# One ring of SBUF slots for all large operands of a cached-attention decode kernel

## The chip, the cores and the metric

The kernel runs on one core of a Trainium2 chip. The metric is the device time of one execution in microseconds (us), lower is better. A time is quoted as the median of some runs. An execution is called slow when it is over 1.5% above the fastest of the same kernel.

Engines: PE is TensorE (PEld its weight loads), DVE is VectorE, ACT is ScalarE, POOL is GpSimd, SP is SyncE, which issues the large loads. "Group" means four batches of one kv head: 1 MB of K and 1 MB of V; there are 16. "The Trainium skill" is a set of notes on the chip; its pages are named by title.

## The reference, cut to what matters

One decode step: layer norm, attention over the last 1024 positions of a cache, a gated FFN beside it, and a product of both added to the input.

```python
B, D, Hq, Hkv, Sk, Dh, F = 8, 512, 32, 8, 4096, 128, 1792      # W = Sk // 4 = 1024
xn = layernorm(x)                                   # x: (8, 1, 512), all bfloat16
q = xn @ wq                                         # wq: (512, 4096)
scores = einsum(q, k[:, :, Sk-W:, :]) * Dh ** -0.5  # four q heads share a kv head
o = einsum(softmax(scores), v[:, :, Sk-W:, :])
s = o @ wo                                          # wo: (4096, 512)
g = silu((gelu(xn @ w_gate) * (xn @ w_up)) @ w_down)
return x + s * g
```

Nothing is used twice: 16 MiB of K, 16 of V, 4 each of wq and wo and 5.25 of FFN weights are read once, 47.46 MB. So the time of the loads is a floor for any version.

## The kernel before

Weights have tiles of their own. K goes through 6 buffers of 256 KB, V through 20. All of K comes first, then all of V; the probabilities of all 64 (head, batch) pairs wait in SBUF between. In both caches a partition takes 8 consecutive positions of one pair, a row of 2 KB.

```python
k_pool = ctx.enter_context(tc.tile_pool(name="k_pool", bufs=6))
v_pool = ctx.enter_context(tc.tile_pool(name="v_pool", bufs=20))
# ... wq, gate, up and down loads; q projection and FFN ...
for hkv in range(Hkv):
    for b in range(B):
        k_sb = k_pool.tile([P, NSC, Dh], BF16, name="k_sb")            # NSC = 8
        nc.sync.dma_start(out=k_sb, in_=A_k_cache[b, hkv, win0:Sk, :]
                          .rearrange("(p c) d -> p c d", c=NSC))
        # 8 transposes into kT_ps (PE), one copy to kT (DVE),
        # 8 score matmuls (PE), one exp into pT_all (ACT)
# 4 matmuls with ones and reductions: the sums of all exps; one reciprocal
for hkv in range(Hkv):
    for b in range(B):
        v_sb = v_pool.tile([P, NSC, Dh], BF16, name="v_sb")
        nc.sync.dma_start(out=v_sb, in_=...)                           # as K
        # 8 matmuls into oT_ps (PE), one product with the reciprocal (DVE)
    nc.sync.dma_start(out=wo_sb[:, hkv * rep : (hkv + 1) * rep, :], in_=...)  # 512 KB
    # 4 matmuls of 512 columns into s_ps
```

The softmax here doesn't subtract the row's maximum and nothing guards it: scores larger than these inputs give would overflow.

## Time and profile before

| what | value | view |
|---|---|---|
| time, median of the first 3 runs | 150.45 us (149.07 to 153.27) | runs |
| HBM read | 47.46 MB, 318 GB/s over the span | page |
| last stage, V and wo | DMA share 1.02 to 1.06, 355 to 385 GB/s | windows |
| K stage, 40 to 90 us | DMA share 0.84 to 1.00, 273 to 349 GB/s | windows |

DMA share is the time of the packets as a share of 16 DMA engines; above 1, packets overlap. The page cuts the span into 40 slices, counted here from 0. A digit is the busy share of a slice in tenths; PEclk is the clock granted to PE, in tenths of full speed; the last row is what the DMA engines moved.

```profile
PE   0000137499988896998998996597474748585760
...
DVE  2100001057296885788788885831211121121213
...
PEclk9999999999999999689999999755555555555555
DMA  4999999957999699889989899999999999999900
GB/s 117 430 419 416 407 403 372 372 161 212 315 390 368 211 342 325 252 278 298 298 321 323 263 311 309 393 372 378 372 380 371 376 357 380 337 386 380 349 30 2
```

There are three stages. Up to 23 us PE waits for wq while the DMA is full. From slice 9 on PE and DVE are busy with K, and the loads mostly drop below 350 GB/s. From slice 25 on V and wo stream with a full DMA, and PE is idle for about a third of the time. SP's waits say why the loads drop in the middle (issuing line, what it waited for, us in total, times, longest):

```profile
SPq L203 <- PE sc_ps L221: 21.0, 31, 1.0
...
SPq L203 <- PE kT_ps L211: 7.7, 19, 1.3
```

K loads wait for the matmuls that free one of six buffers, 28.7 us in all. So the loads are the floor, and they are held back in the K stage. The chain of waits agrees (the chain that ended last, shares of the span; SPq is SyncE's instruction queue, "issue" is time without a visible wait):

```profile
DMA 66%; PE 24%; DVE 5%; issue 3%; SPq 1%
```

### The profile page before, as it was taken

The page shows a single profiled execution, that of the slowest core. Times are in us where ns is not written, and L with a number is a line of the kernel's source. Part 1 is how long each engine was busy: PE and PEld are TensorE (multiplying, and loading weights), DVE is VectorE, ACT ScalarE, POOL GpSimd, SP SyncE. Part 2 cuts the span into 40 slices and gives each one's busy share as a digit, 9 for nine tenths or more (in the row PEclk, how much of TensorE's full clock was granted, in tenths as well). Part 3 has the DMA queues.
Part 4 walks back from the last instruction along what each step waited for, and adds up shares of the span by engine and source line. Part 5 has one row for each costly group of instructions (what it writes and reads, how often), then busy time and mean ns, then how long its engine had stood idle before and what let it go on. Part 6 is the DMA issues. An engine that isn't in the chain of part 4 may idle for free.

```text
span 149.5 us, 4236 instructions
## 1 busy us (share of the span) xinstructions
PE 97.0 (65%) x1830; PEld 73.4 (49%) x1830; DVE 64.2 (43%) x154; ACT 16.5 (11%) x70; POOL 1.4 (1%) x6
## 2 busy tenths in 40 slices
PE   0000137499988896998998996597474748585760
PEld 0000127497466785987876874453433334342420
DVE  2100001057296885788788885831211121121213
ACT  4000000052122221222222221000000000000000
POOL 3000000000000000000000000000000000000000
PEclk9999999999999999689999999755555555555555
DMA  4999999957999699889989899999999999999900
GB/s 117 430 419 416 407 403 372 372 161 212 315 390 368 211 342 325 252 278 298 298 321 323 263 311 309 393 372 378 372 380 371 376 357 380 337 386 380 349 30 2
DMA packets 25843, 47.74 MB, mean 319 GB/s; under 512 B 2256, under 2 KB 8160, under 8 KB 25312
## 3 DMA queue, kind: packets, MB, share of 16 engines
q1 hardware_dynamic: 23216, 41.97, 79.9%
q10 hardware_dynamic: 2336, 3.67, 7.1%
q0 software_dynamic: 272, 1.84, 2.9%
q8 instruction: 14, 0.23, 0.6%
q14 instruction: 5, 0.04, 0.1%
HBM read 47.46 MB, written 0.01 MB: 318 GB/s over the span
## 4 chain that ended last, share of the span: by engine, by line
DMA 66%; PE 24%; DVE 5%; issue 3%; SPq 1%
DMA v_sb<-in_A_v_cache_dram 22%; DMA k_sb<-in_A_k_cache_dram 17%; DMA wq_sb<-in_A_wq_dram 15%; DMA wo_sb<-in_A_wo_dram 12%; PE kT_ps L211 10%; PE s_ps L300 4%; PE sc_ps L221 4%; DVE kT L217 3%; PE qT_ps L135 2%; PE f_ps L181 2%; PE gu_ps L153 1%; SPq L269 1%; DVE tmp L309 0%; DVE out_sb L311 0%; SPq L292 0%
## 5 line engine op out<-in xcount | busy, mean ns | idle before, releaser
L217 DVE COPY kT<-kT_ps 128x1024 bf16<-128x1024 bf16 x64 | 43.6, 690 | 14.4 <-PE kT_ps L211 14.1
L211 PE MATMUL kT_ps<-ident,k_sb 128*128 128x128 bf16 x512 | 41.6, 228 | 3.2 <-DMA k_sb<-in_A_k_cache_dram 3.2
L211 PEld LDWEIGHTS <-k_sb 128*128 128x128 bf16 x512 | 31.3, 102 | 3.8 <-DMA k_sb<-in_A_k_cache_dram 3.8
L284 DVE TENSOR_TENSOR oT_all<-oT_ps,recip_all 128x4 bf16<-128x4 f32 x64 | 11.0, 175 | 36.4 <-PE oT_ps L277 35.4
L277 PE MATMUL oT_ps<-pT_all,v_sb 128*128 128x4 bf16 x512 | 19.9, 167 | 10.2 <-DMA v_sb<-in_A_v_cache_dram 7.3
L277 PEld LDWEIGHTS <-v_sb 128*128 128x128 bf16 x512 | 16.8, 105 | 19.4 <-DMA v_sb<-in_A_v_cache_dram 10.6
L221 PE MATMUL sc_ps<-qT_all,kT 128*128 128x4 bf16 x512 | 22.7, 166 | 3.8 <-DVE kT L217 1.7
L221 PEld LDWEIGHTS <-kT 128*128 128x128 bf16 x512 | 17.9, 97 | 10.0 <-DVE kT L217 8.5
L300 PE MATMUL s_ps<-wo_sb,oT_all 128*8 128x512 bf16 x32 | 14.9, 620 | 8.0 <-DMA wo_sb<-in_A_wo_dram 8.0
L228 ACT ACTIVATE pT_all<-sc_ps 128x32 bf16<-128x32 f32 x64 | 12.6, 197 | 43.9 <-PE sc_ps L221 43.9
L153 PE MATMUL gu_ps<-xnT_sb,wg_sb 128*128 128x8 bf16 x56 | 3.4, 168 | 12.5 <-DMA wg_sb<-in_B_w_gate_dram 10.4
L142 DVE CAST qT_all<-qT_ps 128x64 bf16<-128x64 f32 x4 | 0.9, 225 | 21.3 <-PE qT_ps L135 21.3
L300 PEld LDWEIGHTS <-oT_all 128*8 128x8 bf16 x32 | 3.3, 106 | 12.8 <-issue 10.3
L153 PEld LDWEIGHTS <-wg_sb 128*128 128x128 bf16 x56 | 2.7, 104 | 10.5 <-DMA wg_sb<-in_B_w_gate_dram 10.5
L135 PE MATMUL qT_ps<-xnT_sb,wq_sb 128*128 128x8 bf16 x128 | 3.6, 168 | 3.4 <-DMA wq_sb<-in_A_wq_dram 3.4
L135 PEld LDWEIGHTS <-wq_sb 128*128 128x128 bf16 x128 | 3.5, 104 | 3.5 <-DMA wq_sb<-in_A_wq_dram 3.5
L153 PEld LDWEIGHTS <-wu_sb 128*128 128x128 bf16 x56 | 2.6, 104 | 5.2 <-DMA wu_sb<-in_B_w_up_dram 3.0
L153 PE MATMUL gu_ps<-xnT_sb,wu_sb 128*128 128x8 bf16 x56 | 3.1, 168 | 2.9 <-DMA wu_sb<-in_B_w_up_dram 2.9
L163 ACT ACTIVATE z_381<-gu_ps 128x112 f32<-128x112 f32 x1 | 0.3, 264 | 26.8 <-PE gu_ps L153 26.8
L252 DVE TENSOR_REDUCE sums_sb<-sums_ps 128x64 f32<-128x512 f32 x4 | 2.7, 684 | 1.1 <-PE sums_ps L243 1.1
L181 PE MATMUL f_ps<-wd_sb,hT_sb 128*8 128x512 bf16 x14 | 3.2, 379 | 0.0
L120 PE MATMUL xnT_ps<-ident,xhat 8*128 8x8 bf16 x4 | 0.3, 168 | 4.4 <-DVE xhat L99 4.4
(33 smaller groups left out, 15.9 us busy)
## 6 DMA issues: line engine op xcount, KB each, us to landing
k_sb<-in_A_k_cache_dram SPq DMA_DIRECT2D x64, 256.0 KB, 4.3
v_sb<-in_A_v_cache_dram SPq DMA_DIRECT2D x64, 256.0 KB, 6.1
wq_sb<-in_A_wq_dram SPq DMA_DIRECT2D x1, 4096.0 KB, 22.0
wo_sb<-in_A_wo_dram SPq DMA_DIRECT2D x8, 512.0 KB, 6.2
wg_sb<-in_B_w_gate_dram ACTq DMA_DIRECT2D x1, 1792.0 KB, 14.3
wd_sb<-in_B_w_down_dram ACTq DMA_DIRECT2D x1, 1792.0 KB, 32.1
wu_sb<-in_B_w_up_dram POOLq DMA_DIRECT2D x1, 1792.0 KB, 16.9
x_sb<-in_A_x_dram SPq DMA_DIRECT2D x1, 8.0 KB
```

The lines of the kernel that those rows point to most:

```text
L135: nc.tensor.matmul(qT_ps[:, mi, :], wq_sb[:, k, m * Dh : (m + 1) * Dh], xnT_sb[:, k, :], start=(k == 0), stop=(k == NDC - 1),)
L153: nc.tensor.matmul(gu_ps[:, j, w, :], wsb[:, k, j * 128 : (j + 1) * 128], xnT_sb[:, k, :], start=(k == 0), stop=(k == NDC - 1),)
L181: nc.tensor.matmul(f_ps, hT_sb[:, j, :], wd_sb[:, j, :], start=(j == 0), stop=(j == NFC - 1),)
L211: nc.tensor.transpose(kT_ps[:, c * 128 : (c + 1) * 128], k_sb[:, c, :], ident,)
L217: nc.vector.tensor_copy(out=kT, in_=kT_ps)
L221: nc.tensor.matmul(sc_ps[:, c, :], kT[:, c * 128 : (c + 1) * 128], qg, start=True, stop=True,)
L228: nc.scalar.activation(out=pT_all[:, gi, :, :], in_=sc_ps, func=ACT.Exp, scale=inv_sqrt_dh,)
L252: nc.vector.tensor_reduce(out=sums_sb[:, i * GB : (i + 1) * GB, :], in_=sums_ps.rearrange("p (g c j) -> p g j c", g=GB, c=NSC, j=rep), axi ...
L269: nc.sync.dma_start(out=v_sb, in_=A_v_cache[b, hkv, win0:Sk, :].rearrange("(p c) d -> p c d", c=NSC),)
L277: nc.tensor.matmul(oT_ps, v_sb[:, c, :], pT_all[:, gi, c, :], start=(c == 0), stop=(c == NSC - 1),)
L284: nc.vector.tensor_tensor(out=oT_all[:, hkv * rep : (hkv + 1) * rep, b], in0=oT_ps, in1=recip_all[:, gi, :], op=ALU.mult,)
L300: nc.tensor.matmul(s_ps, oT_all[:, h, :], wo_sb[:, h, :], start=(h == 0), stop=(h == Hq - 1),)
```

## The change

Its intent: keep the DMA queue full from the first to the last byte, with long rows. Every large operand goes through one ring of 22 slots of 1 MB in order of use. A K or V slot holds four batches; partition `r * 4 + i` takes 32 consecutive positions of batch `i`, a row of 8 KB. K and V alternate by group. As a slot mixes four batches, a score matmul gives columns for all four, and exps with a bias of -30000 wipe out the wrong ones, one exp for each batch. FFN weights come in rows of 7 KB with their columns taken at a stride of seven. The output and the FFN's second product are spread over four groups of 32 partitions. The core of the diff, shortened, with cuts at `# ...`:

```diff
-    k_pool = ctx.enter_context(tc.tile_pool(name="k_pool", bufs=6))
-    v_pool = ctx.enter_context(tc.tile_pool(name="v_pool", bufs=20))
+    ring = ctx.enter_context(tc.tile_pool(name="ring", bufs=22))
+    p_pool = ctx.enter_context(tc.tile_pool(name="p_pool", bufs=3))
+    I = 4; R = P // I; C = W // R; CB = 8; NB = C // CB        # C = 32, NB = 4
+    # ...
+    def load_cache(src, g):
+        # ... hkv and b0 from g
+        t = slot()
+        nc.sync.dma_start(out=t, in_=src[b0 : b0 + I, hkv, win0:Sk, :]
+                          .rearrange("i (r c) d -> r i (c d)", c=C))
+    # ...
+    load_k(0); load_wq(); load_k(1); load_v(0); load_k(2); load_v(1); load_ffn()
+    for g in range(3, NG):
+        load_k(g)
+        load_v(g - 1)
+        if g % GW == 0:
+            load_wo(g // GW - 1)
+    load_v(NG - 1)
+    load_wo(NG // GW - 1, parts=2)
+    # ...
+    def score_block(n):        # 8 matmuls of 16 columns; after a group's last block:
+            for i in range(I):
+                nc.scalar.activation(
+                    out=pT[g][:, :, i * rep : (i + 1) * rep],
+                    in_=sc[g][:, :, i * rep : (i + 1) * rep],
+                    func=ACT.Exp, bias=diag[:, i : i + 1], scale=inv_sqrt_dh)
+    def sum_group(g):
+        sums_ps = ps_m.tile([P, C, IR], FP32, name="m_ps")
+        nc.tensor.matmul(sums_ps, ones_pp, pT[g], start=True, stop=True)
+        # reduce, reciprocal (DVE)
+    def value_block(g, s):
+        if s == 0:
+            sum_group(g)
+            oT[g] = ps_m.tile([P, IR], FP32, name="m_ps")
+        # 8 matmuls into oT[g]; after the last block the product with the reciprocal
+    # ...
+    LA = 2
+    for n in range(NG * NB):
+        if n + LA < NG * NB:
+            transpose_block(n + LA)
+        score_block(n)
+        g, s = n // NB, n % NB
+        if g > 0:
+            value_block(g - 1, s)
+        # ... ffn_up() at g == 3, ffn_down() at g == 4, project_out() in two of every four g
```

## The prediction

> **What bounds it now.** Three stages, by the table of windows. Up to 23 us it waits for wq: the DMA moves 378 to 412 GB/s with large rows, PE is nearly idle. From 30 to 86 us it transposes K; only 225 to 349 GB/s flow, because loads wait for one of six K buffers (SyncE's waits: 31 waits, 21.0 us, for the score matmuls, 19 more for transposes), while DVE (7.7 to 8.5 of each 10 us) and PE pace each other: 0.8 us per (head, batch). From 95 to 144 us V and wo stream with the DMA share above 1.0, but at 355 to 385 GB/s. The chain of waits says the same: DMA 66%, PE 24%, DVE 5%. Overall 47.5 MB are read in 149.5 us: 318 GB/s.
>
> **What changes.** The bytes stay. (a) One ring of 22 MB, in order of use: a load waits for the use of a slot 22 loads older, so the queue should never run dry. (b) Rows: the trace's DMA packet records give medians of 46 ns for 1 KB, 84 ns for 2 KB, 275 ns for 7 KB, 319 ns for 8 KB; over 16 engines that is 356, 390, 417 and 411 GB/s. K, V and wq come in 8 KB rows, FFN weights in 7 KB rows; only wo keeps 1 KB. The Trainium skill (DMA: Bandwidth & Descriptors, Rules for kernel authors) asks for 128 partitions and at least 1 MiB per DMA; the 256 KB loads here already kept the share above 1.0 in the V stage, so I credit row length, not DMA size. (c) K and V interleave, so PE and DVE work spreads over the whole stream.
>
> **DMA time.** 37.7 MB at 411 = 91.8 us; FFN 5.5 MB at 417 = 13.2; wo 4.2 MB at 356 = 11.8: 116.8 us.
>
> **Does compute fit?** Per group (2 MiB, 5.1 us of DMA), estimates from trace pitches at full clock: 32 transposes at 57 ns, 32 scores and 32 value matmuls at 28 ns, one sum: about 3.9 us of PE. DVE: four kT copies of 690 ns, one reduce of 684 ns, reciprocal and product about 0.4: 3.85 us. ACT: four exps of about 0.3. All fit, at about 75%. At half clock PE would need some 6.5 us, but it is then continuously busy and should recover full clock, as in the K stage, which ran mostly at 1.0. The FFN's weight columns are now read at a stride of seven; if that slows weight loads to 150 ns, 17 us of PE appear while PE has slack, and the ring hides it.
>
> **Ends.** Head 2.5 us to the first data (x landed then). Tail: today 5.7 us from the last wo landing. Now 16 tiled matmuls (about 1.5), two 128x128 vector operations (0.6 instead of 1.4), four small stores (2.8), semaphore 0.4: about 5.3 us.
>
> **Sum.** 2.5 + 116.8 + 5.3 = 124.6; I say 124.5 us, range 120 to 131. Faster by over 2%: 0.97; same 0.02; slower 0.01.
>
> **Signs.** DMA share near 1.0 and 405 to 420 GB/s in every slice from 3 us to about 119, dips only for wo; SyncE's waits mostly for DMA landings, hardly for PE; the chain nearly all DMA, ending in wo, project-out, store; PE idle but for gaps; PE clock mostly 1.0 after about 40 us.
>
> **What would make it wrong.** 8 KB rows slower because four batches 8 MiB apart are read in turn (then under 400 GB/s at full share); PE or DVE lagging, through a cold clock or strided weight loads, until the ring fills (SyncE waits on PE, DMA share drops); or a backlog of compute after the last landing. Faster, to 120: 8 KB rows above 420 GB/s.

## The result, and the profile after

The changed kernel took 139.34 us (median of 4, 137.75 to 140.10), the kernel before 151.45 us in the same job. The ratio is 0.920, with a 95% interval of 0.910 to 0.931. (A ratio is the mean time of one kernel's fast runs over that of the other's of the same rounds, so not quite the ratio of the medians quoted.) So it is faster, but by less than half of what was predicted: 124.5 us was said, 131 at most.

The profiled run took 140.1 us, and so counts as slow. Nothing below rests on it alone: the profile of e3, a fast run with the same issue order but for the moved FFN, shows the same waits, the same 2.77 us for 24 transposes and about the same pace (6.58 us from sum to sum, mean of six intervals from 90.85 to 130.33 us).

```profile
PE   0486189692006999987696876977596969696960
...
DVE  3443018473003403749374663647283936383741
...
PEclk9999999959555555699868698569755777777775
DMA  3999999999999999999999999999999999200000
GB/s 116 424 429 419 424 419 427 413 423 409 425 422 419 407 376 418 417 417 417 417 386 389 419 422 424 417 417 371 406 417 417 415 414 345 96 5 0 5 0 5
```

The loads do what was predicted. The DMA row is full, the rate is 407 to 429 GB/s but for the slices with wo and their neighbours, and it never runs dry. In the packet records an 8 KB packet took 316 ns on average over all such packets, 415 GB/s over 16 engines. A slice is 3.46 us, so the last load ends in slice 34 (at 120.1 us by the packet records). But the span is 138.3 us, and PE is still at work for most of the rest. The chain of waits has turned over:

```profile
PE 47%; DMA 29%; ACT 10%; DVE 8%; issue 2%; SPq 1%; ACTq 0%
```

DMA fell from 66% to 29%, PE rose from 24% to 47%, and ACT, absent before, has 10%. PE's own waits show what ACT does there (engine, line, what it waited for, us, times, longest):

```profile
PE m_ps L282 <- ACT pT L270: 14.5, 13, 1.4
PE kT_ps L248 <- DMA slot<-in_A_k_cache_dram: 10.0, 2, 9.7
```

L282 is the matmul that sums a group's exps. It waits for them in 13 groups, about 1.1 us each. The second line is one long wait for K 3 while the FFN weights come. The timeline of one group shows the steps (start, duration, engine, line, operation, count, idle time before it). L248 are transposes, L260 scores, L295 values:

```profile
124.73 0.35 PE L295 MATMUL m_ps<-pT,slot 128*128 128x16 bf16 x8
...
124.97 1.14 ACT L270 ACTIVATE pT<-sc_ps,diag 128x128 bf16<-128x128 f32 x4 [5.19 <-PE sc_ps L260]
...
126.16 0.59 PE L282 MATMUL m_ps<-pT,ones_pp 128*128 128x512 bf16 x1 [1.08 <-ACT pT L270]
...
126.54 2.77 PE L248 MATMUL kT_ps<-ident,slot 128*128 128x128 bf16 x24
...
131.36 1.14 ACT L270 ACTIVATE pT<-sc_ps,diag 128x128 bf16<-128x128 f32 x4 [5.25 <-PE sc_ps L260]
...
132.55 0.38 PE L282 MATMUL m_ps<-pT,ones_pp 128*128 128x512 bf16 x1 [1.09 <-ACT pT L270]
```

From sum to sum this group takes 6.39 us; the mean over the 11 intervals from 61.14 to 132.55 us is 6.49. Its loads take about 5.1 us (2 MiB at 415 GB/s). Two things stand out. The sum stands directly behind the last values of the group before, when its exps have just begun. And the 24 transposes behind the sum take 2.77 us, or 107 ns apart (2.77 less one matmul of 0.31, over 23), where the K stage of before had 57 ns (eight weight loads in 0.46 us). The PEclk row shows why: mostly 5 to 8 from slice 10 on. The clock records of this trace alternate between 1.0 and 0.5 in stretches of 3.4, 6.8, 10.2 or 23.9 us.

The program states another order: transposes of two blocks ahead, scores, values, eight by eight, with the sum in front of the first values. But the layer that builds the program may reorder what does not depend on each other. This is what it issues on PE for one group in steady state (from the built program, and the same in the trace; weight loads left out):

```
 1 sum of group g          <- exps of group g
24 transposes of K g+1     (three blocks)
 8 scores   8 transposes   16 scores
24 values of group g
 8 scores                  -> the exps of group g+1 can start
 8 values of group g
 1 sum of group g+1        <- waits for the exps of group g+1
```

### The profile page after: what moved, and what is told of

Read it like the earlier page. It is cut to its first block, busy times and chain, and to the rows that moved or that the text cites. A ratio compares the mean times of both kernels' runs of the same rounds, so it can differ in the third digit from the quotient of the medians.

```text
span 138.3 us, 4349 instructions
## 1 busy us (share of the span) xinstructions
PE 97.6 (71%) x1984; PEld 89.1 (64%) x1984; DVE 64.8 (47%) x135; ACT 21.7 (16%) x70; POOL 1.3 (1%) x8
## 4 chain that ended last, share of the span: by engine, by line
PE 47%; DMA 29%; ACT 10%; DVE 8%; issue 2%; SPq 1%; ACTq 0%
DMA slot<-in_A_k_cache_dram 29%; PE kT_ps L248 22%; ACT pT L270 10%; PE sc_ps L260 7%; PE m_ps L295 6%; DVE kT L252 5%; PE m_ps L282 4%; PE m_ps L333 4%; PE s_ps L317 2%; DVE sums L284 2%; SPq L84 1%; DVE recip L288 1%; SPq L101 0%; DVE tmp L405 0%; DVE out_sb L407 0%
## 5 line engine op out<-in xcount | busy, mean ns | idle before, releaser
L248 PEld LDWEIGHTS <-slot 128*128 128x128 bf16 x512 | 46.0, 130 | 25.1 <-issue 12.7
L248 PE MATMUL kT_ps<-ident,slot 128*128 128x128 bf16 x512 | 52.5, 283 | 10.0 <-DMA slot<-in_A_k_cache_dram 10.0
L270 ACT ACTIVATE pT<-sc_ps,diag 128x128 bf16<-128x128 f32 x64 | 18.4, 368 | 86.3 <-PE sc_ps L260 81.5
L260 PE MATMUL sc_ps<-qT_all,kT 128*128 128x16 bf16 x512 | 21.9, 173 | 2.6 <-DVE kT L252 2.0
L260 PEld LDWEIGHTS <-kT 128*128 128x128 bf16 x512 | 19.7, 102 | 3.8 <-DVE kT L252 3.1
L284 DVE TENSOR_REDUCE sums<-m_ps 128x16 f32<-128x512 f32 x16 | 11.1, 691 | 18.7 <-PE m_ps L282 18.7
L295 PE MATMUL m_ps<-pT,slot 128*128 128x16 bf16 x512 | 18.1, 171 | 0.2 <-issue 0.2
L282 PE MATMUL m_ps<-pT,ones_pp 128*128 128x512 bf16 x16 | 7.6, 476 | 14.6 <-ACT pT L270 14.5
L295 PEld LDWEIGHTS <-slot 128*128 128x128 bf16 x512 | 15.9, 98 | 1.8 <-issue 1.7
L304 DVE TENSOR_TENSOR oT_all<-m_ps,recip 128x16 bf16<-128x16 f32 x16 | 3.6, 228 | 10.3 <-PE m_ps L295 10.2
L228 PE MATMUL m_ps<-xnT_sb,slot 128*128 128x8 bf16 x128 | 4.1, 169 | 4.8 <-DMA slot<-in_A_wq_dram 4.7
L228 PEld LDWEIGHTS <-slot 128*128 128x128 bf16 x128 | 3.7, 104 | 5.7 <-DMA slot<-in_A_wq_dram 5.7
L333 PE MATMUL m_ps<-xpT_sb,slot 128*128 128x8 bf16 x112 | 6.1, 194 | 0.0
L333 PEld LDWEIGHTS <-slot 128*128 128x128 bf16 x112 | 6.1, 152 | 0.0
L288 DVE RECIPROCAL recip<-sums 128x16 f32<-128x16 f32 x16 | 4.0, 252 | 0.5
## 6 DMA issues: line engine op xcount, KB each, us to landing
slot<-in_A_wq_dram SPq DMA_DIRECT2D x4, 1024.0 KB, 11.4
```

Source lines behind the costliest of these rows:

```text
L228: nc.tensor.matmul(q_ps[:, h, :], wq_t[k][:, h * Dh : (h + 1) * Dh], xnT_sb[:, k, :], start=(k == 0 and h == 0), stop=(k == NDC - 1), skip ...
L248: nc.tensor.transpose(t_ps[:, c * P : (c + 1) * P], k_t[g][:, cc * Dh : (cc + 1) * Dh], ident)
L260: nc.tensor.matmul(sc[g][:, s * CB + c, :], kT[n][:, c * P : (c + 1) * P], qT_all[:, hkv, b0 : b0 + I, :], start=True, stop=True,)
L270: nc.scalar.activation(out=pT[g][:, :, i * rep : (i + 1) * rep], in_=sc[g][:, :, i * rep : (i + 1) * rep], func=ACT.Exp, bias=diag[:, i : ...
L282: nc.tensor.matmul(sums_ps, ones_pp, pT[g], start=True, stop=True)
L284: nc.vector.tensor_reduce(out=sums, in_=sums_ps.rearrange("p c m -> p m c"), axis=AX.X, op=ALU.add)
```

## The experiments

Three theories were put against each other. ORDER: the issue order makes PE wait for the exps in every group. CLOCK: PE gets a low clock whatever the order, and that is what costs. IDLE: the 10 us of waiting while the FFN weights come are what is missing at the end. DVE's pace was a further rival. Eleven runs were made, in three jobs on three chips (e1 to e4, e5 to e8, e10 to e12), each with its own runs of the kernel before. Between jobs compare ratios. (The record calls e5 to e8 "unclear" against the kernel before, although their intervals lie below 0.95; three of the seven runs of before in that job were slow.)

| run | us | ratio to before | PE clock, profiled run |
|---|---|---|---|
| changed kernel | 139.34 | 0.920 | 0.759 |
| e1 program order | 127.10 | 0.845 | 0.844 |
| e2 sum late | 128.28 | 0.851 | 0.826 |
| e3 FFN late | 137.32 | 0.913 | 0.780 |
| e4 one exp | 130.08 | 0.866 | 0.841 |
| e5 warm | 131.88 | 0.875 | 0.915 |
| e6 program order, 2 KB rows | 133.88 | 0.888 | 0.856 |
| e7 changed kernel, 2 KB rows | 140.74 | 0.931 | 0.766 |
| e8 program order, no wait for exps | 131.37 | 0.872 | 0.826 |
| e10 sum late, exps twice | 128.82 | 0.855 | 0.811 |
| e11 changed kernel again | 140.11 | 0.927 | 0.712 |
| e12 program order again | 127.37 | 0.845 | 0.855 |

The profiles of e10 and e11, like that of the changed kernel, fell on slow runs. The two fast runs of the changed kernel had clocks of 0.78 and 0.80.

### e1: PE in program order

```diff
+    def mm(*args, **kw):
+        return tc.keep_in_program_order(nc.tensor.matmul(*args, **kw))
+    def tr(*args, **kw):
+        return tc.keep_in_program_order(nc.tensor.transpose(*args, **kw))
-                nc.tensor.matmul(            # every matmul and transpose alike
+                mm(
```

> All TensorE instructions kept in the order in which the program states them (transposes of two blocks ahead, scores, values, eight by eight), nothing else changed. Theory ORDER (the time over the DMA comes from the order in which the built program issues a group: sum behind the last scores, so PE waits for four exps of 1.14 us, then 24 transposes in a lump at a cold clock): the wait of the sum for the exps falls from 14.5 us to under 8, PE's clock stays above 0.85 after 50 us, a group takes about 5 us instead of 6.3, and the time falls to 122 to 130 us. Rival CLOCK (PE gets the low clock whatever the order, because it is idle too often): clock still 0.55 to 0.85, time above 134. Rival DVE pace: DVE busy near 9 of 10 us, time above 132.

Measured: 127.10 us, ratio 0.845 (0.840 to 0.850). No instruction was added or taken away; the results are right. The page and PE's waits:

```profile
PEclk9999999999555555555999999997569999999975
DMA  3999999999999999999999999999999999999600
GB/s 115 388 439 423 417 420 423 425 414 423 409 429 420 420 420 366 412 417 415 417 420 412 394 378 418 425 423 415 417 410 371 406 420 425 415 417 388 213 20 5
```

```profile
PE kT_ps L36 <- DMA slot<-in_A_k_cache_dram: 14.5, 4, 13.7
...
PE m_ps L33 <- ACT pT L276: 5.9, 11, 1.1
```

A slice is now 3.14 us, and the last packet of the loads ends at 120.0 us, where it ended before; the program now ends at 125.6 us instead of 138.3. The wait for the exps is 5.9 us instead of 14.5, and the clock is 9 from slice 19 on but for three slices in the middle and the last two. The mean time from sum to sum is 5.00 us (64.92 to 119.87 us in 11 intervals), the pace of the loads. PE has caught up with the loads again late in the run: the chain of e1 holds a K load from 94.38 us that lands 13.22 us later, and PE waits for it. DVE did the same work (64.7 us busy against 64.8), so its pace was not what bound. ORDER stands, and CLOCK as an independent cause falls: the order alone brought most of the clock back. One part of the expectation failed: the clock was to stay above 0.85 after 50 us, and it was 0.54 from 50 to 60 us and 0.83 in two later stretches of 10 us (1.00 in the other four to 120 us). In the first of these PE was busy nearly all the time, so a PE that is busy by the profile is not enough for full clock (stretch, its length, busy us of PE, PEld, DVE, ACT and POOL, then PEclk, DMA share, GB/s):

```profile
50.00:60.00 10.00, 9.91 (x180) 9.47 (x179) 4.27 (x11) 1.70 (x6) 0.00 (x0) 0.54 1.04 413
```

### e2: the sum stated later

```diff
         if s == 0:
-            sum_group(g)
             oT[g] = ps_m.tile([P, IR], FP32, name="m_ps")
         ...
         if s == NB - 1:
+            sum_group(g)
```

> Only the sum of a group is stated after its value matmuls, so that it no longer stands directly behind the exps; the lump of 24 transposes stays. ORDER, wait part alone: the 14.5 us that the sum waits for the exps go to under 2, and if nothing takes their place the time falls by 10 to 14 us, to 125 to 129. If the lump of transposes at the low clock is the larger part, or the freed wait turns into another one (value matmuls waiting for the exps), it falls by under 6 us, to 134 or more.

Measured: 128.28 us, ratio 0.851 (0.844 to 0.858). In the built program a sum stands in the same place, but it is now that of the group whose values have just ended, not of the group whose exps have just begun; the 24 transposes still come in a lump.

```profile
PE kT_ps L248 <- DMA slot<-in_A_k_cache_dram: 13.3, 2, 13.1
PE sc_ps L260 <- DVE kT L252: 6.5, 19, 0.5
```

No wait of the sum for the exps is left (0.9 us in one place, for values). So the wait, with what follows from it, is enough to explain nearly all of what e1 gained, and the lump of transposes is harmless once PE does not stand still in front of it: from sum to sum it takes 5.12 us (62.20 to 118.50 in 11 intervals).

### e4: one exp in place of four

```diff
-            for i in range(I):
-                nc.scalar.activation(... 128x128 ..., bias=diag[:, i : i + 1], ...)
+            nc.scalar.activation(out=pT[g], in_=sc[g], func=ACT.Exp,
+                                 bias=diag[:, 0:1], scale=inv_sqrt_dh)
```

> One exp over 128x512 with one bias column in place of four of 128x128 (wrong result on purpose; the instruction count of ACT falls by 48). ORDER: the wait of each sum shrinks with the exps, from about 1.15 to about 0.6 us, in some 14 groups: 6 to 9 us less, 130 to 133. CLOCK or DVE: under 3 us less, and the freed time appears as longer transposes.

Measured: 130.08 us, ratio 0.866 (0.858 to 0.873). The order of the built program is that of the changed kernel.

```profile
PE m_ps L281 <- ACT pT L269: 8.3, 13, 0.8
```

The exp takes 0.69 us instead of four of 0.37 that end 1.14 us after the first start, and the sum's wait fell from 14.5 to 8.3 us, 6.2 us. The ratio fell by 0.055, some 8 us, as expected, and the clock was 0.84 in the profiled run, against 0.78 and 0.80 in the fast runs of the changed kernel. The 8 us are more than 6.2, but with an uncertainty of about 2 us they do not show that a shorter wait pays more than its length; e5 tests this. (On purpose this kernel computes the wrong softmax, yet it passed the comparison with the reference, as did e6 and e7. So that comparison cannot tell a right softmax from a wrong one here, and it does not prove the attention of the other kernels right either. The likely reason, not tested, is that the attention enters the output only through a product that is small beside x.)

### e5: useless matmuls in the wait

Here PE's clock is to be changed without touching the order or the wait for the exps.

```diff
         sums_ps = ps_m.tile([P, C, IR], FP32, name="m_ps")
+        # ... s_ps_all is 128x512; s_ps becomes its first 128 columns
+        before = last[0]                       # the last value matmul issued
+        for _ in range(4):                     # from the third group on
+            d = nc.tensor.matmul(s_ps_all[:, P : 4 * P], ones_pp, <128x384 of pT[g - 1]>,
+                                 start=False, stop=False, skip_group_check=True)
+            behind(d, before); before = d      # issue order only
         nc.tensor.matmul(sums_ps, ones_pp, pT[g], start=True, stop=True)   # behind the last
```

> The changed kernel with its issue order as it is, plus four useless 128x384 matmuls (into spare columns of the accumulator's bank) between the last values and each sum, where PE waits about 1.16 us for the exps; results unchanged. Theory CLOCK FOLLOWS IDLENESS (the wait costs twice: itself, and a low clock for the transposes after it, 104 instead of 57 ns each): PE's clock after 60 us rises from about 0.73 to above 0.9, the 24 transposes behind the sum take under 1.7 us instead of 2.5, and the time FALLS, to 127 to 133, though work was added. Rival WAIT ONLY: the clock stays or does not matter; the added 0.64 us (1.28 us at half clock) fit in the wait, so 137 to 141.

Measured: 131.88 us, ratio 0.875 (0.864 to 0.885), against 0.920 of the changed kernel. Work was added, and 0.046 of the time of before, some 7 us, went away. (The order did not stay quite the same: in the trace the sum of two groups now stands behind 16 matmuls of project_out, and that of a third before six transposes. In 11 groups the sum still waits, 5.7 us in all. At some 0.5 us for 16 such matmuls, the two moved sums cannot make up the 7 us.) One group:

```profile
117.56 0.81 PE L295 MATMUL s_ps_all<-pT,ones_pp 128*128 128x384 bf16 x4
117.60 1.14 ACT L271 ACTIVATE pT<-sc_ps,diag 128x128 bf16<-128x128 f32 x4 [4.50 <-PE sc_ps L261]
...
118.79 0.38 PE L302 MATMUL m_ps<-pT,ones_pp 128*128 128x512 bf16 x1 [0.42 <-ACT pT L271]
...
119.01 1.50 PE L249 MATMUL kT_ps<-ident,slot 128*128 128x128 bf16 x24
```

The exps start at 117.60 and the sum at 118.79 us: the wait is as long as it was, but PE works through two thirds of it. Then 24 transposes take 1.50 us instead of 2.77, and PE's clock is 1.00 in every 10 us from 60 to 120 us. The mean time from sum to sum is 5.75 us (61.13 to 124.43 in 11 intervals) against 6.49. So the standstill costs twice: itself, and a half clock for what follows. WAIT ONLY falls. Not separated is whether the useless matmuls helped by ending the standstill or by being large themselves, with 384 columns beside the 16 of scores and values. The Trainium skill (TensorE: Matmul & The Clock Gate, Part 1) describes this gate: half clock by default, full clock after a busy window of about 3.4 us. The stretches of the clock records, multiples of 3.41 us at 0.5 or 1.0, agree.

### e3: the FFN's weights later

```diff
     load_v(1)
-    load_ffn()
     for g in range(3, NG):
         load_k(g)
         load_v(g - 1)
+        if g == 6:
+            load_ffn()
         # ffn_up() at g == 7, ffn_down() at g == 8 instead of 3 and 4
```

> The FFN's 5.25 MB are loaded after K 6 and V 5 instead of before K 3, and the FFN is computed four groups later. Theory IDLE (PE stood idle from 33 to 42.6 us while FFN weights came, and all after that is bound by compute, so those 10 us add to the end): PE's idle there falls to under 3 us and the time falls by 6 to 10 us, to 129 to 133. If the time after 43 us is bound by the loads instead: within 2 us of 139.

Measured: 137.32 us, ratio 0.913 (0.907 to 0.919), which the interval of the changed kernel overlaps. The expectation of IDLE failed in both numbers: the wait for K shrank by 2.5 us only, and the time by 0.007 of before, about 1 us. This meets the number of the rival, within 2 us of 139, but not its reason: that the loads bind after 43 us does not fit e7 below.

```profile
PE m_ps L283 <- ACT pT L271: 14.5, 13, 1.4
PE kT_ps L249 <- DMA slot<-in_A_k_cache_dram: 7.5, 2, 7.2
```

The wait moved to where the weights went, slices 17 and 18 of its page, 58 to 65 us. While 5.5 MB without K or V come, PE runs dry, wherever that is. So IDLE is not a loss that moving the load can give back. The first line, from a fast run, is the wait of the changed kernel again.

### e6 and e7: rows of 2 KB again

```diff
-            out=t,
+            out=t.rearrange("p (i w) -> p i w", i=I),
-            in_=src[b0 : b0 + I, hkv, win0:Sk, :].rearrange("i (r c) d -> r i (c d)", c=C),
+            in_=src[b0 : b0 + I, hkv, win0:Sk, :].rearrange("i (p c) d -> p i (c d)", p=P),
```

In e6 this is done to e1, in e7 to the changed kernel. A load stays 1 MB.

> e1_program_order with the caches' rows of 2 KB again, in the same 1 MB loads (each partition takes 2 KB of each of the four caches; wrong result on purpose, since the mask of the exps no longer fits the layout). 33.6 MB change rows. Theory DMA BOUND after the order is mended: packets of 84 to 93 ns for 2 KB give 352 to 390 GB/s instead of 415, so 5 to 14 us longer than e1: 132 to 141. If e1 is still bound by compute: within 2 us of e1 (127).

> The changed kernel with 2 KB rows in the same 1 MB loads, order untouched (wrong result on purpose). Theory: after 43 us it is bound by the chain of sums, transposes and exps, not by loads, so slower rows cost only what they delay K 3 (about 40 us at 6 to 15 per cent of the part that changes, 10 MB: 2 us): 139 to 143, less than half of what they cost e1. Rival: bound by loads: as much longer as e6 is than e1.

Measured: e6 133.88 us, ratio 0.888 (0.879 to 0.897), so 0.043 of before or 6.5 us over e1. e7 140.74 us, ratio 0.931 (0.917 to 0.945), so 0.011 or 1.6 us over the changed kernel, whose interval it overlaps. The rates of e7:

```profile
DMA  4999999999999999999999999999999999981000
GB/s 82 392 424 430 388 391 386 406 422 418 417 390 388 387 368 375 388 385 387 382 386 374 368 385 386 384 387 381 377 364 385 386 385 391 378 296 66 5 0 5
```

Both kernels' loads slowed alike, from about 418 to about 386 GB/s in the slices of K and V; by the packet records they end at 127.6 us in e7 and 127.5 in e6, 7.5 us later than with 8 KB rows. Yet e7's time hardly moves, while e6's does. This is the mark of what binds: the changed kernel is bound by PE's chain, e1 by its loads. The long rows are worth 6.5 us, but only after the order is mended.

### e8: no wait for the exps at all

```diff
-        if g > 0:
-            value_block(g - 1, s)
+        if n > NB:                                   # one block later
+            value_block((n - NB - 1) // NB, (n - NB - 1) % NB)
         # and sum_group(g) after the group's last values, as in e2
```

> e1_program_order, but each value block is stated one block later and a group's sum after its values, so no matmul should wait for the exps. In e1 PE waited 5.9 us for exps and the last landing was at about 121 us of 125.6, so if e1 is at the floor of its loads: 126 to 128, no gain over e1 (127.1), with the wait gone and PE idle for K instead. If PE still binds: 122 to 125.

Measured: 131.37 us, ratio 0.872, slower than e1 by 0.027 of before. The expectation failed. The wait for the exps is gone, but others came:

```profile
PE m_ps L33 <- issue: 4.1, 3, 1.5
PE m_ps L33 <- DVE sums L290: 3.5, 12, 0.9
```

Values of the next group now wait for a PSUM buffer that the sum's reduction still holds (12 times), and at the end the sum, its reduction and the product follow the last values instead of running beside them: from the start of the last exps to the last projection it takes 3.93 us (121.65 to 125.58) instead of 2.97 in e1 (118.68 to 121.65). The clock was also lower from 60 to 70 us, 0.62 against 1.00. How the 4 us divide among these was not tested.

### e10: the exps twice, off the path

```diff
-            for i in range(I):
+            for i in [j for j in range(I) for _ in range(2)]:    # on e2
```

> e2_sum_late with every exp issued twice (same result), 18 us more of ACT. If it is where the sum stands that makes the exps cost time, and not the exps' length or ACT's share, the doubled exps (2.3 us per group) still end before the values that need them (which start about 3.6 us after the exps do in e2): within 2 us of e2, ratio to before 0.84 to 0.87. If ACT's time counts wherever the sum stands: 13 groups of 1.15 us, 12 us or more over e2.

Measured: 128.82 us, ratio 0.855 (0.849 to 0.860) against 0.851 of e2. Doubling the exps cost nothing that can be told from noise, where shortening them in e4 had gained some 8 us. The order of PE's matmuls in its trace is that of e2. So it is not ACT's load but the place of the sum that counts.

### e11 and e12: both again on one chip

> The changed kernel again, unaltered, to stand on one chip beside e12 and e10: 137 to 141, as before.

> e1_program_order again, unaltered, on one chip with the changed kernel: 126 to 129, 9 to 13 us less than e11, about 7 to 9 per cent.

Measured: 140.11 us (138.64 to 142.36) and 127.37 us (126.72 to 127.74). One of e11's four runs was slow; by fast runs the ratio is 127.30 / 139.62 = 0.912. Program order beats the changed kernel by 9% and the kernel before by 15.5% (ratio 0.845, 0.839 to 0.850).

## Why the prediction was wrong

It was right that the kernel gets faster, and right about the loads. It said 124.5 us, 120 to 131, and the time was 139.3.

- **Loads: right.** Rows of 8 KB were put at 411 GB/s, and 415 were measured; 7 KB at 417 (415 measured); 1 KB at 356 (328 measured, packets of 50 ns instead of 46, worth 1 us; 46 was a median, and the mean of the same packets before was already 49). The last load was to end at 2.5 + 116.8 = 119.3 us. It ended at 120.1 us, with some luck: the first packet came at 1.7 us, and the loads then took 118.4 us.
- **Head and strided weights: right, or harmless.** The 112 matmuls on FFN weights at a stride of seven took 6.1 us, 55 ns each at half clock, not 17 us. (The record of one weight load is 152 ns long, but they overlap.)
- **DVE and ACT: right.** DVE has four copies of 680 ns, 691 + 252 + 228 ns of reduction, reciprocal and product: 3.9 us for a group, as said. ACT has four exps of 0.37 us.
- **The step that failed: "about 3.9 us of PE ... All fit, at about 75%".** It added up pitches of matmuls as if PE never waited inside a group, and took the order in the source for the order of issue. The built program puts the sum only eight value matmuls behind the scores that its exps need, so PE stood still for about 1.1 us in 13 groups. A group took 6.49 us, more than the 5.1 us of its loads. From 43 us on the loads ran ahead, and the end came some 18 us after the last load instead of 5.3. e1 shortens the wait to 5.9 us and e2 takes it away; they give 127 and 128 us.
- **The second half of that step: "it is then continuously busy and should recover full clock".** PE was not continuously busy, as the standstill came in 13 of the 16 groups. The clock flipped between full and half. e5 shows that this part alone costs about 7 us.
- **What was named as a risk came, by another road.** "PE or DVE lagging, through a cold clock or strided weight loads, until the ring fills" was listed; the lag came from an order that the prediction had not looked at. Of the signs given, the PE clock was not "mostly 1.0", and the chain was not "nearly all DMA". SP's waits on PE were a bad sign: the longest were 11.4 us in the changed kernel and 11.1 us in e1, both with a full DMA all the same.

With the order mended the sum of the prediction holds within 3 us: 127.1 against 124.6. Most of the rest is that the sum counted the profile's span, while the device time is 1.8 us longer (127.39 against 125.6 us in e1's profiled run). Within the span e1's last packet ended at 120.0 us, 119.3 said, and the tail took 5.6 us, 5.3 said.

What stays open: why the clock falls at a standstill of only 1.1 us was not settled, nor why it stayed at 0.54 in e1 from 50 to 60 us with PE busy for 9.91 of 10 us. In e2 the same lump of transposes and scores runs mostly at full clock without the standstill, but how much idle time in a window is too much was not measured.

## What to carry to other kernels

When a kernel is to be bound by its loads, compute per group must fit in the groups' time with its waits, not only by the sum of its instructions: look at what each engine's next instruction in the built order waits for, and do not trust the order in the source. A repeated short standstill of PE may cost twice, as it can drop the clock of what follows. And if faster loads gain nothing, slow them down on purpose: if the time does not move either, the gain is waiting behind something else.

## What the Trainium skill lacked or had wrong

- TensorE: Matmul & The Clock Gate, "Why this matters for your kernels", asks for no idle gaps above about 3 us between bursts. Here standstills of 1.1 us, one in each 6.4 us, with matmuls of 16 columns around them, went with a clock that flips to half; filling them with useless matmuls (e5) brought it from 0.78 and 0.80 to between 0.90 and 0.915 (means of the fast runs), and the ratio to before from 0.920 to 0.875. The page also tells of short idles between groups of matmuls that make the clock oscillate ("A second HAM failure mode: psum-queue depth-cycling"), but gives no length for them.
- The same page, Part 4, says that full clock does not engage for PE transposes. Here runs of 24 transposes took 1.50 us with the clock granted at 1.00 (e5), and 2.77 us at half clock. Whether transposes alone would bring the clock up was not tested.
- Perfetto Trace Analysis, "Optimization Strategy", says of consistent bubbles that they can mean too little SBUF or PSUM. The bubble here came 13 times, 14.5 us in all, and shrank to 5.9 us (e1) or went away (e2) with no buffer added, by issuing the sum elsewhere. Apart from a warning about sequences on the vector engine (DVE: scalar operands, raw-bit mode, write accounting and state across instructions), no page was found that says that the order in which a built program issues may differ from the source and must be checked.
- DMA: Bandwidth & Descriptors, "Rules for kernel authors", asks for 1 MiB or more per DMA, and its specifications put full rate at 512 B and more. With 1 MB loads in both cases, rows of 2 KB gave about 386 GB/s and rows of 8 KB about 418 by slices (e7 and the changed kernel); by the mean time of a packet it was 366 and 415, and 328 for wo's 1 KB. The length of a row counted, above 512 B too. The same page ("Why small descriptors are slow") names a fixed cost per packet, and Perfetto Trace Analysis ("DMA Optimizations") advises going from 2 KB to 4 or 8 KB; neither gives a rate for these sizes.
